# A gated mix of sliding-window attention and a token-mixing MLP: another order of the same work on the five engines

## The chip, the cores and the metric

The kernel runs on one core of a Trainium2 chip. The metric is the device time of one execution in microseconds. The core has five engines with a queue of instructions each: TensorE (PE; its weight loads are listed as PEld), ScalarE (ACT), VectorE (DVE), GpSimd (POOL) and SyncE (SP), which in this kernel only issues transfers. They wait for each other with semaphores.

## The reference

The input x has 2048 tokens of 512 features. Two branches are mixed by a gate of each token (all in bf16):

```
g = sigmoid(sum(x * gate_w))                     # one number a token
a = attention(x): qkv = x @ wqkv, 32 heads of 16; query i sees keys i-255 .. i
    o = softmax(q k / 4) v;  a = o @ wo
b = mixer(x): h = layernorm(x)                   # over the 512 features
    u = gelu(h^T w1 + b1)                        # 2048 tokens -> 1376
    y = u w2 + b2                                # 1376 -> 2048 tokens, transposed back
out = g * a + (1 - g) * b
```

## The kernel before

All work is cut into tasks of one engine each (class `Task`), some 1136 in all. A table, `PLAN`, lists for each engine the names of its tasks in the order in which that engine runs them; a digit or letter after a colon is the buffer that the task takes (one character for each). So `s2.v2:06` is a score task that writes the PSUM bank pairs 0 and 6, and `v9.0:3` starts a chain in bank 3. The function `arrange` (line 103 on) merges the five lists into one program with a clock of assumed durations (`cost_of`, line 91). Those durations change no engine's order. They do set one thing in the program: near its end, the kernel lets a POOL task wait for DVE's last operation of the kind that is marked `two`, if that one ended by the planner's clock less than a microsecond before the POOL task starts.

The names, as the prediction uses them:

- `x0.0` and so on, `xt1`, `wqk0` to `wqk3`, `wv`, `gw`, `bias`, `w1_gi`, `w2_f`, `wo`: loads on SP. `xt` are loads that transpose (line 498). `w2` lies in the same buffer as `w1`, so a `w2` load waits for the last `u` step that reads what it overwrites (line 1315). `vs` and `vz` copy values between partitions, SBUF to SBUF (lines 756 and 766); there are three `vz` buffers.
- `q`, `k`, `v`, `u`, `y`: accumulation chains of TensorE (line 708). `q0_1.2` is the step that begins with the third matmul of the chain for head group 0 and token block 1. A step is two matmuls of 512 columns, apart from the first block's q and k (one matmul) and the ends of `y`. `u` needs `h` and `w1`, `y` needs gelu's output, `w2`, and in its last two steps the attention's result.
- `kc`, `vc`, `qc`, `ub`: what takes those chains out of PSUM, on ACT or DVE.
- `s_j.v0` to `v3` and `s_j.C`: scores of block j of 128 queries, 32 rows a tile (lines 980 and 1080; C are the corners of the window). Each writes two bank pairs, and two exponentials, `e_j...0` and `.1` (ACT, line 932, 128x1024 each), empty them. `m_j...` multiplies an exponential with its mask, on DVE (lines 1012, 945) or POOL (line 571).
- `pv_j.0` to `.3`: scores times values, 32 columns a tile (line 1125). `n1_j` to `n4_j` on DVE transpose and normalise its result (`n1`, line 1216, frees the bank pair); in the plan they are written without the line, as `n11` for block 1.
- `gelu`: one stretch of four instructions on ACT (lines 1291 and 1293), with a table load before and after. `f` writes the gated result of a y chain (lines 473, 476), `o` stores it (line 1343).
- `pow`, `h`, `gl`, `gatee`, `ez`: the layer norm and the gate.

TensorE runs in four tilings: the full array for chains, 32 rows for `s`, 32 x 64 for `C`, 32 columns for `pv`. A chain may also be run in 32-column tiles (four matmuls for one). The set `THEN` names the `s` and `pv` tasks after which the chain steps stay in that tiling.

Of the kernel before, what the change touches and what calls it, by code (L numbers as in the profile page):

```python
# [90 lines left out]
def cost_of(t, e):  # L91
    c, n = t.engines[e], t.name
    if e == "PE":
        return c - 0.02 if t.mode == "s" else c * 0.738 if t.mode == "c" else c
    if e == "DVE":
        return max(0.1, c - 0.06)
    if e == "ACT":
        return c - 0.085 if n[:2] in ("vc", "kc", "ub") else c - 0.008 if n[0] == "e" else c
    if e == "POOL" and n[0] == "m" and ".C" in n:
        return c * 1.14  # L100
    return c


def arrange(tasks):
# [21 lines left out]
    while len(order) < len(tasks):  # L126
# [80 lines left out]
    pv=(7, 6, 5, 4, 3),  # L207
# [11 lines left out]
        warm:5 xta0.0.1:4 xta0.0.0:3 warmb xta0.1.1:4 xta0.1.0:5 q2_0.0:6 q3_0.0:0 k1_0.0:2 k3_0.0:3  # L219
        k0_0.0:1 q1_0.0:5 q1_0.1 k2_0.0:7 q0_0.0:4 k2_0.1 q2_0.1 k0_0.1 q0_0.1 k3_0.1 k0_0.2 q0_0.2 k1_0.1  # L220
        q0_0.3 k3_0.2 q1_0.2 k3_0.3 q1_0.3 q3_0.1 q2_0.2 k1_0.2 q1_0.4 k1_0.3 q0_0.4 k0_0.3 k3_0.4 q2_0.3
        k0_0.4 q3_0.2 q2_0.4 k2_0.2 k1_0.4 k2_0.3 k2_0.4 v1.0:1 q3_0.3 q3_0.4 s0.v0:24 v1.2 v0.0:7 q3_1.0:6
        v0.2 q3_1.2 s0.C:24 v5.0:0 k2_1.0:7 k2_1.2 v5.2 s-1.C:24 v3.0:6 v14.0:7 v14.2 s1.v3:04 biast:3 v3.2
        q1_1.0:7 q1_1.2 s1.v0:02 v2.0:6 v2.2 v12.0:4 v12.2 v4.0:5 v4.2 pv-1.0:0 s0.v1:26 k3_1.0:4 k3_1.2
        k3_2.0:5 s1.v2:06 k3_2.2 v6.0:2 q0_1.0:3 q0_1.2 v6.2 pv0.0:0 pv0.1 pv0.2 s1.v1:46 v7.0:3 v7.2
        v15.0:2 s2.v1:06 v15.2 k0_2.0:5 v13.0:4 k0_2.2 v13.2 k1_1.0:3 s1.C:06 k2_2.0:2 k2_2.2 k1_1.2
        s2.v3:06 k0_1.0:5 k0_1.2 v10.0:2 v10.2 pv1.0:0 pv1.1 pv1.2 pv1.3 s2.v0:46 pv1.4 v8.0:2 v8.2 v9.0:3
        v9.2 s2.v2:06 q2_1.0:5 k1_2.0:4 q2_1.2 s2.C:20 k1_2.2 u0.0:6 u0.2 v11.0:7 v11.2 s3.v1:40 u0.4 u0.6
        u0.8 s3.C:02 u2.0:7 u0.10 u2.2 u0.12 u2.4 s3.v2:42 pv2.0:0 u0.14 pv2.1 pv2.2 pv2.3 u2.6 u2.8
        s3.v0:24 u1.0:6 u1.2 u1.4 s3.v3:02 u1.6 u1.8 u2.10 s4.v0:42 u2.12 u1.10 u2.14 u1.12 u1.14 s4.v1:04  # L230
        pv3.0:2 pv3.1 pv3.2 pv3.3 u3.0:7 u3.2 u3.4 s5.v2:04 u3.6 u3.8 u3.10 s4.v3:20 u3.12 u3.14 u4.0:6 u4.2
        s4.v2:24 q0_2.0:7 q0_2.2 u4.4 s4.C:40 u4.6 u4.8 u4.10 s6.v0:02 u4.12 q3_2.0:7 u4.14 pv4.0:4 pv4.1
        pv4.2 pv4.3 s5.v0:02 u5.0:6 q3_2.2 u5.2 u5.4 s5.v1:42 u5.6 u5.8 q2_2.0:7 q2_2.2 s5.C:02 u5.10 u5.12
        u5.14 s6.C:04 u6.0:7 u6.2 u6.4 s6.v2:02 u6.6 u6.8 q1_2.0:6 q1_2.2 u6.10 s5.v3:04 u6.12 u6.14 u7.0:6
        s6.v1:02 u7.2 u7.4 pv5.0:4 pv5.1 pv5.2 pv5.3 s6.v3:02 u7.6 u7.8 k3_3.0:7 k3_3.2 s7.v0:04 u7.10
        pv6.0:2 pv6.1 u7.12 pv6.2 pv6.3 s7.v1:04 u8.0:7 u7.14 u8.2 s7.v3:02 u8.4 k1_3.0:6 k1_3.2 s7.C:04
        u8.6 u8.8 q0_3.0:6 s7.v2:42 q0_3.2 u8.10 u8.12 u8.14 s8.v3:20 u9.0:6 u9.2 u9.4 s8.C:04 u10.0:7 u10.2
        u10.4 s8.v1:24 u9.6 u9.8 u10.6 u9.10 s8.v0:20 u9.12 u10.8 u9.14 s8.v2:42 u10.10 pv7.0:0 pv7.1
        q1_3.0:6 u10.12 u10.14 q1_3.2 s10.v0:24 pv7.2 k2_3.0:7 k2_3.2 pv8.0:2 pv8.1 k0_3.0:6 pv8.2 pv8.3
        pv7.3 k0_3.2 q2_3.0:4 q2_3.2 q3_3.0:5 y4.0:6 y0.0:7 q3_3.2 s9.v1:02 y0.2 y0.4 y4.2 y4.4 y0.6 y4.6  # L240
        y0.8 y0.10 s9.v3:40 y0.11 y0.13 y4.8 s9.v2:02 y4.10 y4.11 y2.0:7 y2.2 s9.C:40 y2.4 y4.13 y2.6
        s9.v0:24 y2.8 y2.10 y7.0:6 y2.11 s10.C:04 y2.13 y7.2 y7.4 s10.v3:02 y7.6 y8.0:7 y8.2 s11.v3:04 y8.4
# [12 lines left out]
    """,
    ACT="""
        xtc0.0.1 xtc0.0.0 kc3_0 kc0_0 kc1_0 kc2_0 e0.v0.0:5 e0.v0.1:4 vc0 vc1 e0.C.0:3 e0.C.1:2 kc2_1 vc5
        e-1.C.1:9 e-1.C.0:8 vc14 e1.v3.0:1 e1.v3.1:b e1.v0.0:a e1.v0.1:0 vc12 gatee0 vc4 e0.v1.1:8 e0.v1.0:9
        e1.v2.0:6 e1.v2.1:7 kc3_1 vc6 e1.v1.1:2 e1.v1.0:3 e2.v1.1:4 e2.v1.0:5 vc15 kc0_2 e1.C.0:d e1.C.1:c
        kc2_2 e2.v3.0:8 vc13 e2.v3.1:9 vc10 kc1_1 e2.v0.1:0 e2.v0.0:b vc8 e2.v2.0:1 e2.v2.1:7 e2.C.1:a kc1_2  # L260
        e2.C.0:d e3.v1.1:c e3.v1.0:6 e3.C.1:e e3.C.0:f e3.v2.1:0 e3.v2.0:b ub0 e3.v0.0:7 e3.v0.1:1 e3.v3.1:a
        e3.v3.0:5 e4.v0.0:4 e4.v0.1:d ub2 e4.v1.0:1 e4.v1.1:0 ub1 gatee2 e5.v2.0:c e5.v2.1:5 e4.v3.0:6
        e4.v3.1:f e4.v2.1:e e4.v2.0:7 e4.C.1:8 e4.C.0:9 e6.v0.1:2 e6.v0.0:3 e5.v0.1:4 e5.v0.0:d e5.v1.1:0
        gatee1 e5.v1.0:1 e5.C.0:7 e5.C.1:6 e6.C.0:e ub5 e6.C.1:f e6.v2.0:a e6.v2.1:b e5.v3.0:8 e5.v3.1:g
        e6.v1.0:9 e6.v1.1:h ub6 e6.v3.0:6 e6.v3.1:7 e7.v0.0:8 e7.v0.1:g kc3_3 e7.v1.0:a e7.v1.1:6 e7.v3.0:f
        e7.v3.1:b e7.C.1:e e7.C.0:7 e7.v2.1:9 e7.v2.0:h e8.v3.1:4 e8.v3.0:5 e8.C.1:c e8.C.0:d e8.v1.0:2
# [1146 lines left out]
```

## Time and profile before

| | |
|---|---|
| three runs | 199.55, 199.56, 199.9 us; median 199.56 |
| the profiled execution | 199.2 us, its span 197.5 us |
| PE busy | 187.4 us, 95% (4008 matmuls recorded, 4040 weight loads) |
| ACT busy | 169.9 us, 86% |
| DVE busy | 157.8 us, 80% |
| POOL busy | 64.6 us, 33% |
| matmuls of chains, 512 columns, one | 380 ns from start to end; the next starts 215 ns after it |
| exponential, 128x1024, one | 1.04 us from start to end |
| DMA | 22.01 MB, most of it in the first 42 us; HBM read 15.6 MB |

The profile is one execution. A line of the chain, of the waits or of the timeline names the engine, the line of the kernel, and what is written and read (`out<-in`). In the timeline the columns are the start, the length, engine and line, operation, form and count, and in brackets the idle time before it with what ended it; neighbours of one kind are merged into one row, and the length then reaches from the first start to the last end. Matmuls overlap, so their lengths do not add up; the time from one start to the next does. Some matmul records are missing.

### The profile page before, as it was taken

To read this page: it belongs to the slowest core of one execution; us is meant where nothing else is said; L and a number is where in the kernel's file an instruction comes from. 1 tells how busy PE (TensorE), PEld (TensorE's weight loads), DVE (VectorE), ACT (ScalarE), POOL (GpSimd) and SP (SyncE) were. 2 spreads that over 40 slices of the span, in tenths; PEclk is the share of its full clock that TensorE was granted. 3 is DMA by queue.
4 is the path that set the end of the run, shared out by engine and by line. 5 is a ranking of instruction groups with operands and counts; after the bars stand their busy time and mean duration, and the time that the engine had idled before them with its cause. 6 is when DMAs were issued, how large, how long until landed. Compare 5 with 4: busy or idle time off the path is not lost.

```text
span 197.5 us, 9026 instructions
## 1 busy us (share of the span) xinstructions
PE 187.4 (95%) x4008; PEld 92.3 (47%) x4040; DVE 157.8 (80%) x340; ACT 169.9 (86%) x200; POOL 64.6 (33%) x102
## 2 busy tenths in 40 slices
PE   7999999999999999999999999899999999999994
PEld 3544344444535344456444563335345354454663
DVE  2699998799999897984767899177955775779893
ACT  3059998999899997999999899998998989899910
POOL 8922796563001122235200420222362320004520
PEclk9999999999999999999999999999999999999999
DMA  5986999942052811001496017001031002003022
GB/s 147 306 212 125 236 328 346 317 123 63 7 156 69 275 62 37 0 3 36 134 391 256 3 39 211 0 5 56 3 109 36 27 9 68 3 3 89 3 98 65
DMA packets 23444, 22.01 MB, mean 111 GB/s; under 512 B 7950, under 2 KB 21518, under 8 KB 23406
## 3 DMA queue, kind: packets, MB, share of 16 engines
q1 hardware_dynamic: 23406, 21.44, 36.1%
q8 instruction: 31, 0.51, 1.1%
q14 instruction: 7, 0.06, 0.1%
HBM read 15.61 MB, written 2.10 MB: 90 GB/s over the span
## 4 chain that ended last, share of the span: by engine, by line
PE 79%; ACT 11%; DVE 4%; issue 3%; DMA 2%; SPq 0%; ACTq 0%
PE pb L708 57%; PE ps L1125 10%; PE ps L980 9%; ACT et L932 7%; PE ps L1080 2%; ACT VA L640 2%; DMA wqkv<-in_A_wqkv_dram 2%; DVE stats L808 1%; ACT L932 1%; DVE et L1216 1%; DVE zt L1233 0%; SPq L489 0%; ACT ug L1291 0%; DVE h L824 0%; PE ps L1036 0%
## 5 line engine op out<-in xcount | busy, mean ns | idle before, releaser
L932 ACT ACTIVATE et<-ps 128x1024 bf16<-128x1024 f32 (+1 forms) x104 | 98.8, 1011 | 8.2 <-PE ps L980 5.5
L571 POOL TENSOR_SCALAR_AFFINE_SELECT et<-et 128x512 bf16<-128x512 bf16 (+3 forms) x60 | 41.6, 704 | 98.4 <-ACT et L932 65.7
L932 ACT ACTIVATE XT<-ps 128x1024 bf16<-128x1024 f32 (+1 forms) x50 | 49.1, 1028 | 1.2 <-PE ps L980 0.7
L708 PEld LDWEIGHTS <-wb 128*32 128x32 bf16 (+4 forms) x663 | 32.5, 97 | 37.0 <-issue 7.0
L708 PE MATMUL pb<-ug,wb 128*32 128x512 bf16 (+6 forms) x344 | 43.9, 365 | 0.9 <-issue 0.6
L708 PE MATMUL pb<-h,wb 128*32 128x512 bf16 (+2 forms) x301 | 41.9, 380 | 1.7 <-issue 1.7
L708 PE MATMUL pb<-XT,wqkv 128*128 128x512 bf16 (+2 forms) x166 | 31.8, 369 | 1.2 <-issue 0.8
L980 PE MATMUL ps<-QZ,KT 32*128 32x256 bf16 (+1 forms) x496 | 23.1, 265 | 0.9 <-ACT et L932 0.8
L1125 PEld LDWEIGHTS <-VA 128*32 128x32 bf16 (+1 forms) x1056 | 20.3, 97 | 6.2 <-issue 1.6
L792 DVE TENSOR_TENSOR QZ<-pb,par 128x1024 bf16<-128x1024 f32 x16 | 19.1, 1213 | 3.3 <-PE pb L708 2.4
L1125 PE MATMUL ps<-et,VA 128*32 128x128 bf16 (+2 forms) x760 | 21.7, 217 | 0.0
L1216 DVE STREAM_TRANSPOSE et<-ps 128x1024 f32<-128x1024 f32 (+1 forms) x13 | 15.7, 1207 | 4.2 <-PE ps L1125 3.7
L1012 DVE TENSOR_TENSOR et<-et,mask 128x512 bf16<-128x512 bf16 x38 | 16.9, 454 | 2.7 <-ACT et L932 2.7
L708 PEld LDWEIGHTS <-wqkv 128*128 128x128 bf16 (+1 forms) x172 | 12.0, 97 | 13.7 <-DMA wqkv<-in_A_wqkv_dram 0.9
L571 POOL TENSOR_SCALAR_AFFINE_SELECT XT<-XT 128x512 bf16<-128x512 bf16 (+1 forms) x15 | 9.8, 659 | 24.5 <-ACT XT L932 13.5
L708 PE MATMUL pb<-wo,xo 128*32 128x512 bf16 (+3 forms) x152 | 17.5, 369 | 0.4 <-issue 0.3
L980 PEld LDWEIGHTS <-KT 32*128 32x128 bf16 x496 | 7.4, 92 | 21.7 <-ACT et L932 12.1
L708 PE MATMUL pb<-wqkv,XT 128*128 128x512 bf16 x60 | 15.8, 380 | 0.6 <-issue 0.3
L1012 DVE TENSOR_TENSOR XT<-XT,mask 128x512 bf16<-128x512 bf16 x20 | 9.7, 485 | 6.4 <-ACT XT L932 6.4
L808 DVE BATCH_NORM_STATS2 stats<-xo 128x6 f32<-128x512 bf16 x16 | 10.6, 675 | 4.2 <-DMA xo<-in_A_x_dram 4.2
L1125 PEld LDWEIGHTS <-VZ 128*32 128x32 bf16 x832 | 13.2, 97 | 0.4
L1125 PE MATMUL ps<-XT,VA 128*32 128x128 bf16 (+2 forms) x296 | 12.7, 217 | 0.1
(77 smaller groups left out, 201.7 us busy)
## 6 DMA issues: line engine op xcount, KB each, us to landing
wb<-in_B_w_dram SPq DMA_DIRECT2D x18, 512.0 KB, 6.6
VZ<-VA SPq DMA_DIRECT2D x26, 70.0 KB, 2.5
xo<-in_A_x_dram SPq DMA_DIRECT2D x3, 512.0 KB, 5.0
wb<-in_B_w_dram SPq DMA_DIRECT2D x4, 352.0 KB, 7.5
out_dram<-ot SPq DMA_DIRECT2D x11, 128.0 KB, 1.8
wqkv<-in_A_wqkv_dram SPq DMA_DIRECT2D x4, 256.0 KB, 5.4
xo<-in_A_x_dram SPq DMA_DIRECT2D x2, 256.0 KB, 2.9
wqkv<-in_A_wqkv_dram SPq DMA_DIRECT2D x1, 512.0 KB, 7.7
```

The lines of the kernel that those rows point to most:

```text
L571: return nc.gpsimd.affine_select(out=out_, in_=in_, pattern=[[0, n] for n in pattern] + [[step, HB]], compare_op=op, fill=0.0, base=base_, ...
L640: return nc.scalar.activation(out_(), in_(), ACT.Copy)
L708: made.append(nc.tensor.matmul(buf(b)[c:z_, c0:c0 + w_], lhsT=lhsT[:, c:z_], rhs=rhs, start=(j == 0), stop=(j == n - 1), skip_group_check= ...
L792: lambda k=k, b=b: nc.vector.tensor_tensor(out=QZ[:, k, :, (i % NQ) * SB:(i % NQ + 1) * SB], in0=buf(b)[:, None, :].to_broadcast([P, 2, SB ...
L808: f"bs{t_}", {"DVE": 0.67}, lambda b=b, t_=t_: nc.vector.bn_stats(buf(b)[:], xo[:, t_, :]),
L932: lambda e=e, b=b, shape=shape: nc.scalar.activation(out=shape(buf(e)), in_=shape(buf(b)), func=ACT.Exp, scale=SCALE),
L980: made.append(nc.tensor.matmul(to[:, :, done:done + m], lhsT=keys(j if x == "A" else j - 1, k)[rows], rhs=q[rows], start=True, stop=True, ...
L1012: made.append(nc.vector.tensor_tensor(out=v, in0=v, in1=m.to_broadcast(list(v.shape)), op=ALU.mult))
L1080: made.append(nc.tensor.matmul(buf(b2[r // 2])[m_:m_ + HB, at:at + P], lhsT=keys(t_, k)[rows, a:a + HB], rhs=q[rows], start=True, stop=Tru ...
L1125: return lambda: nc.tensor.matmul(to(), lhsT=v() if callable(v) else v, rhs=buf(e)[rows, col:col + n], start=first, stop=last, tile_positi ...
L1216: lambda: nc.vector.transpose(out=view(buf(tr).bitcast(FP32)), in_=view(buf(o))), [last], takes=[tr], uses=[o],
```

## The change

All five lists, the buffers in them and the set `THEN` are replaced. No task is added or removed, and none changes its instructions, but 72 tasks change their engine: 33 masks go from DVE to POOL and 21 from POOL to DVE; 10 tasks go from ACT to DVE (`xtc0.0.1 xtc0.0.0 vc14 vc15 ub5 kc3_3 f1 f9 f12 f15r`) and 8 from DVE to ACT (`xtc0.1.0 xtc0.1.1 vc3 vc2 kc3_2 vc7 ub4 f14`). The lists then have 500 tasks on PE, as before; 192 on ACT (194 before), 283 on DVE (293), 87 on POOL (75) and 74 on SP. Two assumed durations of the planner change. The order of the score and pv tasks is the same but for `s5.v0`, which moves ahead of `pv4`, `pv7.3`, which moves ahead of `pv8.0`, and `pv10` and others by single chain steps.

The diff, cut to what is spoken of:

```diff
-        return c - 0.02 if t.mode == "s" else c * 0.738 if t.mode == "c" else c
+        return c - 0.01 if t.mode == "s" else c * 0.738 if t.mode == "c" else c
...
     PE="""
-        warm:5 xta0.0.1:4 xta0.0.0:3 warmb xta0.1.1:4 xta0.1.0:5 q2_0.0:6 q3_0.0:0 k1_0.0:2 k3_0.0:3
-        k0_0.0:1 q1_0.0:5 q1_0.1 k2_0.0:7 q0_0.0:4 k2_0.1 q2_0.1 k0_0.1 q0_0.1 k3_0.1 k0_0.2 q0_0.2 k1_0.1
-        q0_0.3 k3_0.2 q1_0.2 k3_0.3 q1_0.3 q3_0.1 q2_0.2 k1_0.2 q1_0.4 k1_0.3 q0_0.4 k0_0.3 k3_0.4 q2_0.3
-        k0_0.4 q3_0.2 q2_0.4 k2_0.2 k1_0.4 k2_0.3 k2_0.4 v1.0:1 q3_0.3 q3_0.4 s0.v0:24 v1.2 v0.0:7 q3_1.0:6
...
-        q1_3.0:6 u10.12 u10.14 q1_3.2 s10.v0:24 pv7.2 k2_3.0:7 k2_3.2 pv8.0:2 pv8.1 k0_3.0:6 pv8.2 pv8.3
-        pv7.3 k0_3.2 q2_3.0:4 q2_3.2 q3_3.0:5 y4.0:6 y0.0:7 q3_3.2 s9.v1:02 y0.2 y0.4 y4.2 y4.4 y0.6 y4.6
-        y0.8 y0.10 s9.v3:40 y0.11 y0.13 y4.8 s9.v2:02 y4.10 y4.11 y2.0:7 y2.2 s9.C:40 y2.4 y4.13 y2.6
...
+        warm:5 xta0.0.0:7 xta0.0.1:3 warmb xta0.1.0:3 xta0.1.1:5 k1_0.0:1 q0_0.0:0 q2_0.0:7 q2_0.1 k2_0.0:4
+        q1_0.0:2 k1_0.1 k2_0.1 q0_0.1 k0_0.0:3 q0_0.2 k1_0.2 k0_0.1 q1_0.1 k2_0.2 k1_0.3 q1_0.2 q0_0.3
+        q0_0.4 k0_0.2 q1_0.3 q1_0.4 k1_0.4 q3_0.0:6 q2_0.2 q3_0.1 k0_0.3 k0_0.4 k2_0.3 k3_0.0:5 k3_0.1
+        q2_0.3 q2_0.4 k2_0.4 k3_0.2 q3_0.2 s0.v0:20 q3_0.3 q3_0.4 k3_0.3 k3_0.4 v1.0:4 biast:3 v0.0:2 v0.2
...
+        pv7.0:2 pv7.1 u10.12 u10.14 k2_3.0:6 k2_3.2 s10.v0:04 pv7.2 q2_3.0:7 q2_3.2 pv7.3 pv8.0:0 k0_3.0:6
+        pv8.1 pv8.2 pv8.3 q1_3.0:3 q3_3.0:2 k0_3.2 q1_3.2 q3_3.2 y4.0:4 y0.0:5 s9.v1:06 y0.2 y4.2 y0.4 y0.6
+        y0.8 y0.10 y4.4 y0.11 s9.v3:26 y4.6 y0.13 y4.8 s9.v2:02 y4.10 y4.11 y2.0:5 y4.13 s9.C:60 y2.2 y2.4
...
     ACT="""
-        xtc0.0.1 xtc0.0.0 kc3_0 kc0_0 kc1_0 kc2_0 e0.v0.0:5 e0.v0.1:4 vc0 vc1 e0.C.0:3 e0.C.1:2 kc2_1 vc5
...
-        e8.v1.1:3 e8.v0.0:0 e8.v0.1:1 gatee3 e8.v2.1:8 e8.v2.0:a ub10 e10.v0.0:6 e10.v0.1:9 gelu e9.v1.0:8
...
+        xtc0.1.0 xtc0.1.1 kc1_0 kc0_0 kc2_0 e0.v0.0:a kc3_0 e0.v0.1:5 vc0 e0.C.0:9 e0.C.1:b vc1 vc2
...
+        e8.v3.0:d e8.C.0:e e8.C.1:f e8.v1.0:8 e8.v1.1:9 e8.v0.1:g e8.v0.0:h e8.v2.1:4 e8.v2.0:7 ub10
+        e10.v0.0:3 e10.v0.1:1 gelu e9.v1.1:f e9.v1.0:e e9.v3.0:0 e9.v3.1:2 e9.v2.0:d e9.v2.1:c e9.C.0:7
...
     POOL="""
-        ident masks ones blanks pow0 m0.v0.1 m0.v0.0 m-1.C.0 m-1.C.1 m0.C.1 pow1 m1.v3.1 m0.C.0 m0.v1.0
-        m0.v1.1 m1.v0.1 m1.v2.0 m1.v3.0 m1.v1.1 m1.v0.0 m1.C.1 m1.v2.1 m2.v1.1 m2.v3.0 pow2 pow3 m2.v2.0
...
+        ident blanks ones masks m0.v0.1 m-1.C.0 m-1.C.1 m1.v3.0 m1.v3.1 m0.v0.0 m0.C.1 pow1 m0.C.0 m1.v0.1
+        m0.v1.0 m0.v1.1 m1.v2.1 pow0 pow2 m1.v0.0 m1.v1.1 m1.v1.0 m1.v2.0 m2.v1.1 pow3 m2.v0.1 m2.v2.0
...
     SP="""
-        x0.0 x0.2 wqk0 wqk1 wqk2 x1.4 wqk3 gw wv xt1 bias xt3 vs0 x2.8 vs1 xt2 w1_21 x3.12 w1_00 w1_01 w1_10
-        w1_02 w1_20 vs2 w1_23 w1_12 w1_11 vz4:1 w1_03 vz8:0 vz2:2 vz3:2 w1_13 w1_22 vz5:2 wo w2_0 w2_3 vz6:1
-        vz11:2 vz7:1 w2_1 w2_4 w2_2 w2_7 w2_6 w2_5 w2_8 vz10:0 w2_9 w2_10 vz9:1 o2 o4 o7 o0 o8 vz13:1 vz12:0
...
+        x0.0 x0.2 wqk0 wqk1 wqk2 wqk3 bias gw wv xt1 x1.4 xt3 w1_03 x2.8 vs0 xt2 w1_21 vs2 vs1 w1_12 w1_00
+        x3.12 vz2:1 w1_13 vz6:2 w1_20 w1_01 w1_11 w1_02 w1_10 vz3:0 w2_0 vz7:1 w2_1 vz4:0 w2_3 w2_2 vz5:0 wo
+        w1_22 w1_23 w2_7 vz8:2 w2_4 w2_6 w2_5 vz10:0 w2_8 vz9:1 w2_9 w2_10 o4 vz11:2 o2 o0 vs13 o8 o7 o1
...
-            lambda fc=fc, fsz=fsz: nc.sync.dma_start(w2[:fsz, fc, :], B_w2[fc * P:fc * P + fsz, :]), gone, lat=2.9,
+            lambda fc=fc, fsz=fsz: nc.sync.dma_start(w2[:fsz, fc, :], B_w2[fc * P:fc * P + fsz, :]), gone, lat=3.2,
```

## The prediction

> **What bounds the kernel now.** I read the page first (engines' share, the chain that ended last), then the waits of TensorE, then timelines of the places where TensorE waits.
>
> ```profile
> span 197.5 us, 9026 instructions
> PE 187.4 (95%) x4008; PEld 92.3 (47%) x4040; DVE 157.8 (80%) x340; ACT 169.9 (86%) x200; POOL 64.6 (33%) x102
> PE 79%; ACT 11%; DVE 4%; issue 3%; DMA 2%; SPq 0%; ACTq 0%
> L932 ACT ACTIVATE et<-ps 128x1024 bf16<-128x1024 f32 (+1 forms) x104 | 98.8, 1011 | 8.2 <-PE ps L980 5.5
> ```
>
> TensorE carries 79% of the last chain. Busy time alone does not say whether it works or drains, so I worked its time out from the starts. The first chain matmul starts at 5.82 and the last ends near 194.6. A 512-column matmul follows the one before it after 0.2155 us; four 32-column ones of a tiled step share that time. In such units the kernel has 608 for the projections, u and y (131.0 us) and 35.5 us of scores and score-times-value products: 166.5. At 119.50 and 119.83 below, a score step of 0.2155 is followed after 0.33: a change of tiling costs 0.11. The order has 165 changes; each measured that way, they make 18.8 us. That leaves about 3 us, half of it scattered gaps of hundredths. TensorE really waits for only about 1.6 us after 5.82:
>
> ```profile
> 5.82 3.98 PE L708 MATMUL pb<-XT,wqkv 128*128 128x256 bf16 x25 [0.23 <-DMA wqkv<-in_A_wqkv_dram]
> 9.99 2.75 PE L708 MATMUL pb<-XT,wqkv 128*128 128x512 bf16 x12 [0.19 <-issue]
> ...
> 42.82 0.40 PE L980 MATMUL ps<-QZ,KT 32*128 32x256 bf16 x8 [0.16 <-ACT et L932]
> ...
> 119.50 0.40 PE L980 MATMUL ps<-QZ,KT 32*128 32x256 bf16 x8
> 119.83 3.54 PE L708 MATMUL pb<-ug,wb 128*128 128x512 bf16 x15
> 123.75 0.40 PE L980 MATMUL ps<-QZ,KT 32*128 32x256 bf16 x8 [0.38 <-ACT et L932]
> ```
>
> The waits I find: 0.15 near 9.7 (the fourth weight block), 0.2 at 29.6 (pv0.1 waits for a mask), 0.15 at 32.2, 0.22 at 42.8 (s2.v2 waits for the transpose n11 to free its bank), 0.12 at 122.4, 0.46 at 123.75 and 0.1 at 125.6 (after gelu), some 0.2 more. ScalarE is the partner: two exponentials follow each score step, one every 0.905 us, and in most visits TensorE's next score step starts 0.05 to 0.3 us after the exponential that frees its bank. So the two run in lock step, with no stock of slack: a later exponential, mask or copy shows on TensorE at once. The clock column of the page is 9 throughout.
>
> **What the Trainium skill says.** "TensorEngine Tiling (Array Packing)", Tiling Modes: changing the tiling mode drains TensorE; the trace agrees, at 0.11 us a change. "GPSIMD Engine Reference", Specifications: GpSimd shares its SBUF interfaces with VectorE. The trace shows POOL waiting 8.5 us for a DVE mask (L571 <- DVE et L1012), but that can be the wait the program itself puts in. "DMA: Bandwidth & Descriptors", Queues, rings and completion order: an engine's descriptors are consumed in ring order. It agrees: the packets of the fourth weight block land among and behind those of x1.4, issued just before it. "ScalarE: Activation LUTs", What ACT_TABLE_LOAD costs: back-to-back ACTIVATEs overlap by about 93 ns; the trace has 1.04 us an exponential and a pitch of 0.905.
>
> **The change part by part.** Matmuls and bytes are the same in both. The lines of `cost_of` and the `lat` of 3.2 emit nothing; they only shift the planner's clock, which decides the merging and where a POOL operation gets a wait for VectorE. What remains is order, placing and buffers.
>
> *Changes of tiling.* Counting the order with `THEN`: 165 becomes 164; tiled chain steps 72 becomes 73. -0.11 us.
>
> *Start.* The loads up to wqk2 are unchanged, so 5.82 stays. wqk3 goes ahead of x1.4 (0.5 MB, at the 306 GB/s of that slice of the page up to 1.7 us earlier), and TensorE asks for it at about 8.6: the 0.15 wait goes. Bound 0 to 0.25. The four bias loads now stand ahead of gw, wv and the transposing load xt1 on SP's queue (1.5 us of issue, 12.67 to 14.14), x1.4 after it. That load occupied the queue for 7.11 us, most of it waiting; with less ahead of it wv still lands by about 12.6, and v1.0 wants it at 13.3. 0.
>
> *First exponentials.* s0.v0 comes after 36 chain steps instead of 41 (four of 0.2155 and one of 0.431 less), at about 12.2 instead of 13.63; its copies kc1, kc0, kc2 end by 12.5, so ScalarE starts its exponentials near 12.6, not 14.08. By s1.v0 both orders have 56 chain steps, and from there on the count before every visit is equal or one step off. ScalarE's copies move too: vc2, vc3, vc7, kc3_2, ub4 to it; vc14, vc15, ub5, kc3_3 from it. From e0.v0 to s1.v1 its sum is 1.43 us more than in the old order, TensorE's 1.29 more. Against the start that is earlier by 1.4, ScalarE stands at +0.1 there, at about -0.3 before gelu.
>
> *Masks.* 33 go from DVE to POOL, 21 back: 12 x 0.336 less on DVE, 12 x 0.617 more on POOL (from the pitch of each engine's masks). With the copies and f1, f9, f12, f15r, DVE's queue is 3.2 us shorter in all. At n11 it is 0.84 ahead: the 0.22 wait at 42.8 should go (0 to 0.22). On POOL the critical stretch is from the corner masks m-1.C to m0.v1.1, which pv0.1 waits for:
>
> ```profile
> 20.69 4.32 POOL L571 TENSOR_SCALAR_AFFINE_SELECT et<-et 64x512 bf16<-64x512 bf16 x6 [2.61 <-ACT VA L640]
> 25.09 0.20 POOL L818 TENSOR_TENSOR rstd<-mv,eps 128x4 f32<-128x4 f32 x1
> 25.37 1.02 POOL L819 TENSOR_TENSOR rstd<-rstd,half 128x4 f32<-128x4 f32 x1
> 26.36 5.20 POOL L571 TENSOR_SCALAR_AFFINE_SELECT et<-et 128x512 bf16<-128x512 bf16 x8
> ```
>
> Before, 8.4 us of POOL work without a pause brought m0.v1.1 to 29.05. After, m1.v3.0, m0.v0.0 and m1.v0.1 stand in that stretch too: 10.2 us. e-1.C should end near 18.8 instead of 20.6, so m0.v1.1 starts at 29.0 again, and ends near 29.7. TensorE, 0.15 to 0.25 earlier, just waits longer: the gain of the start is lost here. I book -0.15 for the start and +0.15 here; bounds: 0 to +1.85 if POOL starts no earlier. The new masks after 45 us I book at nothing: POOL was busy for 0.2 to 4 of each 10 us, and m8.v1.1 or m15.A.1 end one microsecond or more before their pv step. If that cover were gone, each late mask costs 0.62.
>
> *Queue of transfers.* vz6 (waits for vc7, near 33) stands ahead of w1_20, w1_01, w1_11, w1_02 and w1_10 on SP. Those 2.4 MB take some 8 us at the 300 GB/s of those slices and are in by 42; u0.4 wants w1_01 at 47.5. 0. w1_22 and w1_23 go behind vz5, near 76; u8.8 wants them at 98. w2_9 and w2_10 go behind vz9, which is free two microseconds sooner because pv7.3 moves ahead of pv8.0; w2_10 was issued at 117.8 and used at 122.4 with a wait of 0.12, which should go. -0.12.
>
> *Gelu.* Its table load, 6.5 us of work and second load follow e10.v0, and s9.v3 waits for the first exponential behind them. Seven and a half chain steps stand between s9.v1 and s9.v3 in both, so the 0.46 moves with ScalarE alone: gatee3 (0.17) leaves this stretch, and ScalarE is some 0.3 ahead: -0.2, bounds -0.46 to +0.4.
>
> *After gelu.* ScalarE loses three f (0.78 each); the two or three waits of 0.1 may go: -0.1. The number of chain steps between visits is the same or one off; where s14.v1, s14.C and s15.A come one step earlier the bank is free by n113, whose queue is 2.5 us shorter.
>
> *Tail.* From pv15.2 to y15l.11 TensorE has 2.5 us of steps in both, and the chain n115 to n415 takes 2.2. f15m and o15m end it unchanged. 0.
>
> Sum: -0.11 - 0.15 + 0.15 - 0.22 - 0.12 - 0.2 - 0.1 = -0.75. Every one of some 75 visits gets a new bank or neighbour in a lock step with no slack; for new waits of the sort already seen (0.1 to 0.2, two of them) I add 0.25, an estimate. So -0.5: the profiled execution goes from 199.2 (197.5 span and 1.7 around it) to 198.7. The median of the runs is 199.56, 0.36 above it; so I predict 199.05.
>
> **The rivals.** *Nothing gained:* ScalarE and POOL hold TensorE at the mask of pv0.1 and at gelu at the same moments as before, and what TensorE saves between them it waits. For it: the slack of hundredths. Against: n11 and w2_10 don't hang on them. 199.45. *Slower, by POOL:* the ordering puts 1.84 us more POOL work ahead of m0.v1.1. If m-1.C starts no earlier than at 20.69, as it would if ScalarE's early start is lost to a copy or to a bank, m0.v1.1 ends at 31.5, pv0.1 waits 1.85 us more, and nothing gives it back: 201.2. It decides from about 19.5 on; each microsecond later is one more. *Everything gained:* all 1.6 us of waits go, and 197.9 is left; but the gelu wait hangs on work that isn't changed.
>
> **How the numbers follow.** Small gain 0.47, everything 0.04, nothing 0.22, slower by POOL or a wait like it 0.27. A measurement here can tell 0.2% (0.4 us) from no change: faster 0.51, same 0.22, slower 0.27. Range 198.1 to 200.9: it drops the floor and the full price of the slower case, which most likely comes in part, at 200 to 201. The small gain's own range is 198.3 to 199.2.
>
> **What would show it.** Right: first exponential near 12.6; no wait before the fourth block; m-1.C on POOL near 18.9 and pv0.1 held near 29.9; s2.v2 with no wait for n11; s9.v3 near 123.4. Wrong: m-1.C at 20 or later; waits of half a microsecond at visits that had 0.1; wqk1 late for TensorE's new order.

## The result: slower, and the profile after

The kernel after takes 200.35 us (median of 19 runs), the one before 199.9 beside it: a ratio of 1.0026, interval 1.0015 to 1.0037. The forecast was 199.05 and a small gain. In the profiled executions it is 200.44 us with a span of 198.7, against 199.2 with a span of 197.5.

The page of the kernel after, first its span, then the engines, then the chain that ended last by engine:

```profile
span 198.7 us, 9038 instructions
PE 188.0 (95%) x4007; PEld 92.2 (46%) x4040; DVE 154.6 (78%) x330; ACT 169.0 (85%) x198; POOL 74.5 (37%) x113
PE 70%; ACT 10%; DMA 5%; SPq 5%; DVE 4%; issue 3%; POOL 1%; ACTq 0%; POOLq 0%; DVEq 0%
```

The work is where the order put it: VectorE has 3.2 us less and POOL 9.9 us more. TensorE's busy time tells nothing, so I read the starts of single tasks out of both traces and subtracted. The third column is a mended version of the kernel after, described below.

| stretch of TensorE | before | after | mended |
|---|---|---|---|
| to the first chain matmul | 5.82 | 6.11 | 6.11 |
| from there to s1.v0 | 15.88 | 16.50 | 15.97 |
| s1.v0 to pv0.2 | 8.39 | 8.54 | 8.16 |
| pv0.2 to s2.v2 | 12.73 | 12.77 | 12.77 |
| s2.v2 to s10.v0 | 69.60 | 69.59 | 69.59 |
| s10.v0 to s9.v3 | 11.33 | 11.33 | 11.32 |
| s9.v3 to the last chain step | 70.57 | 70.72 | 70.73 |
| last chain step | 194.32 | 195.56 | 194.65 |

Of the 1.24 us between the profiles, 0.91 are there at s1.v0 and 1.06 at pv0.2. Behind 44 us only 0.15 are lost, after gelu.

The timeline of TensorE in the kernel after, at its start (start, length, engine, line, operation, form, count; in brackets the idle time before the row and what ended it):

```profile
6.11 0.50 PE L708 MATMUL pb<-XT,wqkv 128*128 128x256 bf16 x3 [0.19 <-DMA wqkv<-in_A_wqkv_dram]
7.21 5.46 PE L708 MATMUL pb<-XT,wqkv 128*128 128x256 bf16 x30 [0.59 <-ACT XT L640]
```

Three chain steps run, then TensorE stands until 7.21. The third of them began at 6.34 and takes 0.11, so the fourth, q2_0.1, waits 0.76 us: for ScalarE's copy xtc0.1.0. The timeline of ScalarE before and after:

```profile
0.79 1.28 ACT L640 ACT_TABLE_LOAD   x1 [0.79 <-PEq L1397]
4.32 1.09 ACT L640 ACTIVATE XT<-pb 128x512 bf16<-128x512 bf16 x2 [2.25 <-PE pb L646]
```

```profile
5.26 1.28 ACT L640 ACT_TABLE_LOAD   x1 [5.26 <-DVE XT L641]
6.56 1.08 ACT L640 ACTIVATE XT<-pb 128x512 bf16<-128x512 bf16 x2
```

The first block above is before, the second after. ScalarE's first table load, 1.28 us, used to run while the first loads were on their way. Now a wait for VectorE's copies (DVE XT L641) stands in front of it, and the copy that TensorE asks for at 6.45 begins at 6.56. "Perfetto Trace Analysis", Identifying Dependency Chains, in the Trainium skill, says that an instruction with several conditions may get event instructions with the other waits ahead of it. The trace agrees: a semaphore instruction of ScalarE, 17 ns long, ends at 5.23 and the table load follows.

The timeline of POOL after, which answers the one shown of before:

```profile
19.91 6.16 POOL L571 TENSOR_SCALAR_AFFINE_SELECT et<-et 64x512 bf16<-64x512 bf16 x9 [2.66 <-ACT et L932]
26.16 0.20 POOL L818 TENSOR_TENSOR rstd<-mv,eps 128x4 f32<-128x4 f32 x1
26.44 1.02 POOL L819 TENSOR_TENSOR rstd<-rstd,half 128x4 f32<-128x4 f32 x1
27.42 2.13 POOL L571 TENSOR_SCALAR_AFFINE_SELECT et<-et 64x512 bf16<-64x512 bf16 x3
29.50 1.27 POOL L571 TENSOR_SCALAR_AFFINE_SELECT XT<-XT 128x512 bf16<-128x512 bf16 x2
```

The corner masks m-1.C begin at 19.91; m0.v1.1 is the second of the last row, at 30.12: a stretch of 10.2 us without a pause, against 8.4 before. TensorE runs into its end:

```profile
30.20 0.41 PE L1125 MATMUL ps<-et,VA 128*32 128x128 bf16 x16
30.44 0.22 PE L1125 MATMUL ps<-XT,VA 128*32 128x128 bf16 x2
30.82 0.40 PE L1125 MATMUL ps<-XT,VA 128*32 128x128 bf16 x14 [0.16 <-POOL XT L571]
```

pv0.1 starts at 30.44 with two matmuls, and the other fourteen come at 30.82, behind the mask.

### The profile page after: what moved, and what is told of

The parts are those of the page before. It is cut to its first block, busy times and chain, and to the rows that moved or that the text cites. A ratio compares the mean times of both kernels' runs of the same rounds, so it can differ in the third digit from the quotient of the medians.

```text
span 198.7 us, 9038 instructions
## 1 busy us (share of the span) xinstructions
PE 188.0 (95%) x4007; PEld 92.2 (46%) x4040; DVE 154.6 (78%) x330; ACT 169.0 (85%) x198; POOL 74.5 (37%) x113
## 4 chain that ended last, share of the span: by engine, by line
PE 70%; ACT 10%; DMA 5%; SPq 5%; DVE 4%; issue 3%; POOL 1%; ACTq 0%; POOLq 0%; DVEq 0%
PE pb L708 51%; PE ps L1125 9%; PE ps L980 8%; DMA xo<-in_A_x_dram 5%; ACT et L932 4%; ACT ug L1291 2%; PE ps L1080 2%; SPq L757 2%; SPq L498 2%; ACT XT L932 2%; SPq L521 1%; SPq L756 1%; DVE stats L808 1%; ACT L932 1%; ACT L1291 1%
## 5 line engine op out<-in xcount | busy, mean ns | idle before, releaser
L932 ACT ACTIVATE et<-ps 128x1024 bf16<-128x1024 f32 (+1 forms) x97 | 90.9, 999 | 8.0 <-PE ps L980 4.5
L932 ACT ACTIVATE XT<-ps 128x1024 bf16<-128x1024 f32 x57 | 55.9, 1039 | 4.0 <-PE ps L980 2.4
L708 PEld LDWEIGHTS <-wb 128*32 128x32 bf16 (+3 forms) x651 | 32.3, 97 | 35.5 <-issue 6.3
L708 PE MATMUL pb<-ug,wb 128*32 128x512 bf16 (+5 forms) x348 | 44.0, 367 | 1.1 <-issue 0.9
L708 PE MATMUL pb<-h,wb 128*32 128x512 bf16 (+1 forms) x285 | 42.7, 380 | 1.4 <-issue 1.4
L571 POOL TENSOR_SCALAR_AFFINE_SELECT XT<-XT 128x512 bf16<-128x512 bf16 (+1 forms) x28 | 20.0, 723 | 47.8 <-ACT XT L932 38.9
L1125 PE MATMUL ps<-et,VA 128*32 128x128 bf16 (+2 forms) x688 | 19.4, 216 | 0.3 <-ACT et L932 0.3
L1012 DVE TENSOR_TENSOR et<-et,mask 128x512 bf16<-128x512 bf16 x28 | 12.6, 457 | 3.0 <-ACT et L932 3.0
L476 DVE TENSOR_SCALAR ot<-pb,c,c 128x512 bf16<-128x512 f32 (+2 forms) x12 | 8.9, 746 | 6.7 <-PE pb L708 6.7
L945 DVE TENSOR_TENSOR et<-et,mask 128x1024 bf16<-128x1024 bf16 (+1 forms) x16 | 11.4, 721 | 1.2 <-ACT et L932 1.2
(75 smaller groups left out, 199.5 us busy)
```

Of the source, the lines that this page charges most:

```text
L476: return nc.vector.tensor_scalar(out=out_, in0=in_, scalar1=scale, scalar2=bias, op0=ALU.mult, op1=ALU.add)
L571: return nc.gpsimd.affine_select(out=out_, in_=in_, pattern=[[0, n] for n in pattern] + [[step, HB]], compare_op=op, fill=0.0, base=base_, ...
L708: made.append(nc.tensor.matmul(buf(b)[c:z_, c0:c0 + w_], lhsT=lhsT[:, c:z_], rhs=rhs, start=(j == 0), stop=(j == n - 1), skip_group_check= ...
L932: lambda e=e, b=b, shape=shape: nc.scalar.activation(out=shape(buf(e)), in_=shape(buf(b)), func=ACT.Exp, scale=SCALE),
L945: return nc.vector.tensor_tensor(out=v, in0=v, in1=m[:, None, :].to_broadcast([P, n, w]), op=ALU.mult)
L1012: made.append(nc.vector.tensor_tensor(out=v, in0=v, in1=m.to_broadcast(list(v.shape)), op=ALU.mult))
```

## The experiments

Every ratio is to the kernel before on the same chip. Its medians there were 199.67 us for the first four runs, 199.56 for the control, the bank, the masks on top of it and the loads back, 199.6 for the masks alone and the attempts to beat both kernels, and 199.5 for the last run. The plan's lines in the edits are cut at their ends.

### The start

Theory: the table load behind a wait, and with it q2_0.1, is the loss. Rivals: the other order of the loads makes the first weight block land later (6.07 against 5.77 in the first two profiles); or the masks and the lock step of TensorE and ScalarE set the time whatever the start.

**Copies back.**

```diff
-        xtc0.1.0 xtc0.1.1 kc1_0 kc0_0 kc2_0 e0.v0.0:a
+        xtc0.0.1 xtc0.0.0 kc1_0 kc0_0 kc2_0 e0.v0.0:a
-        const zeros bs0:0 xtc0.0.1 xtc0.0.0 ba0 bs2:1 bs1:0 parity ba2 bs3:1
+        const zeros bs0:0 ba0 bs2:1 bs1:0 parity ba2 xtc0.1.0 xtc0.1.1 bs3:1
```

> The kernel after, with the four copies of the first block exchanged back (xtc0.0.1, xtc0.0.0 on ACT, xtc0.1.0, xtc0.1.1 on DVE, as before the change). Theory, start (ACT's table load stands behind a wait for DVE's copies, and q2_0.1 waits 0.76 us for it): the table load is at 0.8 again, xtc0.1.0 runs on DVE at 6.0 to 6.4, q2_0.1 starts at 6.5 to 6.6 instead of 7.21, and the 0.6 reaches the end: about 199.7 where the kernel after has 200.35. Rival, loads (the weights land later for the new order of loads): the first chain matmul stays at 6.1, and of the loss 0.3 stays. Rival, masks and lock step (the order behind the start sets the time): TensorE waits what it saves, at pv0.1 or later, and the time is 200.1 to 200.4.

Measured: 200.04, 1.0019 (0.9997 to 1.0041). The table load is at 0.80 and q2_0.1 has no wait of its own. But in the profiled execution the first weight block landed at 6.94, the first chain matmul came at 6.99, and the end was no earlier than after (195.53). So only some 0.3 of the median came back (200.35 to 200.04, on two chips), less than the theory's 0.6, and the landing was seen to scatter.

**Early table.**

```diff
+    add("early", {"ACT": 1.4}, lambda: nc.scalar.activation(early[:], half[:], ACT.Copy), [k0])
-        xtc0.1.0 xtc0.1.1 kc1_0 kc0_0 kc2_0 e0.v0.0:a
+        early xtc0.1.0 xtc0.1.1 kc1_0 kc0_0 kc2_0 e0.v0.0:a
```

> The kernel after, with one tiny ACT operation (128x4, of a constant) ahead of xtc0.1.0, so that the table load needs no DVE copy. All copies stay where the change put them. Theory, start: table load near 1.0, xtc0.1.0 on ACT at about 5.45 to 6.05, q2_0.1 at about 6.45 with no wait worth naming; the 0.76 reaches the end: 199.6. If the place of the copies itself (0.60 on ACT against 0.42 on DVE) and not the table load is what costs: xtc0.1.0 still ends near 7.1, time 200.3. Rival, masks and lock step: q2_0.1 is early and the time stays at 200.1 to 200.4.

Measured: 200.1, 1.002 (1.0 to 1.004). The load is at 0.80, the copy at 6.02, q2_0.1 at 6.84. About 0.25 came back, not 0.76; the chain steps from 6.20 to 7.43 took 0.21 us each and not 0.11 (see the last section). The first weight block landed at 5.73 here, with the new order of loads.

**The exchange alone, in the kernel before.**

```diff
-        xtc0.0.1 xtc0.0.0 kc3_0 kc0_0
+        xtc0.1.0 xtc0.1.1 kc3_0 kc0_0
-        zeros bs0:0 ba0 bs3:1 const bs1:0 parity ba3 xtc0.1.0 xtc0.1.1 ba1
+        zeros bs0:0 xtc0.0.1 xtc0.0.0 ba0 bs3:1 const bs1:0 parity ba3 ba1
```

> The kernel before, with the exchange of the four copies alone (xtc0.1.0, xtc0.1.1 on ACT, xtc0.0.1, xtc0.0.0 on DVE). Theory, start: the table load moves from 0.79 to about 5.3, xtc0.1.0 ends near 7.15, q1_0.1, the seventh chain step, starts at 7.2 instead of 6.60, and the kernel before becomes 0.4 to 0.7 slower. Rivals (loads; masks and lock step): no more than 0.2 slower, the second since the 0.15 wait for the fourth weight block, the mask of pv0.1 and gelu would absorb it.

Measured: 199.51, 1.0002 (0.9982 to 1.0022): no loss, against my theory. Its timelines of ScalarE and of POOL:

```profile
0.79 1.28 ACT L640 ACT_TABLE_LOAD   x1 [0.79 <-PEq L1397]
5.60 1.08 ACT L640 ACTIVATE XT<-pb 128x512 bf16<-128x512 bf16 x2 [3.53 <-PE pb L646]
```

```profile
16.72 1.28 POOL L571 TENSOR_SCALAR_AFFINE_SELECT et<-et 128x512 bf16<-128x512 bf16 x2 [5.74 <-DVE junk L860]
20.62 4.31 POOL L571 TENSOR_SCALAR_AFFINE_SELECT et<-et 64x512 bf16<-64x512 bf16 x6 [2.62 <-DVE junk L860]
```

Two things follow. The exchange doesn't put the table load behind a wait; something that came with it does. What differs is the PSUM bank: in this run ScalarE's first copy reads bank 5, which no other engine had to empty; in the kernel after it reads bank 3, which VectorE's copy had to empty first. And the kernel before has a reserve at its start: TensorE began 0.21 later here and s0.v0 was at 13.90 instead of 13.63, yet m-1.C stands at 20.62 (20.69 before), because POOL waits there for VectorE's gate work, not for the exponential. The view of before names a copy on ScalarE (ACT VA) for this wait, but in this run that copy ends at 20.93, when the mask already runs; the mask starts 0.13 behind the end of the gate work in both, and again in the kernel before with `const` first (below). After, m-1.C follows e-1.C.0 by 0.07 us, so a late start goes through. The reserve is small: with `const` first s0.v0 came 0.58 later in the kernel before, VectorE was late too, m-1.C stood at 21.20, and 0.35 reached the last chain step.

**The loads alone, in the kernel before.**

```diff
-        x0.0 x0.2 wqk0 wqk1 wqk2 x1.4 wqk3 gw wv xt1 bias xt3
+        x0.0 x0.2 wqk0 wqk1 wqk2 wqk3 bias gw wv xt1 x1.4 xt3
```

> The kernel before, with the first order of loads of the kernel after alone (wqk3 and the bias loads ahead of gw, wv and xt1, x1.4 behind xt1). Theory, start: the first chain matmul stays within 0.15 of 5.82, the wait of 0.15 for the fourth weight block goes, time the same or 0.15 less. Rival, loads: the first weight block lands at 6.07 and the first chain matmul is at 6.1; time 0.1 to 0.3 more.

Measured: 208.47, 1.0439 (1.0412 to 1.0467), which nobody expected. Its timelines of VectorE and of TensorE:

```profile
17.09 1.29 DVE L808 BATCH_NORM_STATS2 stats<-xo 128x6 f32<-128x512 bf16 x2 [9.30 <-DMA xo<-in_A_x_dram]
18.29 0.17 DVE L812 BATCH_NORM_AGGREGATE mv<-stats 128x2 f32<-128x6 f32 x1
18.49 0.69 DVE L808 BATCH_NORM_STATS2 stats<-xo 128x6 f32<-128x512 bf16 x1
19.10 3.47 DVE L792 TENSOR_TENSOR QZ<-pb,par 128x1024 bf16<-128x1024 f32 x3
```

```profile
21.58 0.61 PE L980 MATMUL ps<-QZ,KT 32*128 32x256 bf16 x8 [7.64 <-DVE QZ L792]
```

VectorE's order has the layer norm of x1.4 ahead of the copies of q. With x1.4 behind the transposing load it waits 9.3 us, and s0.v0 waits for q: it comes 7.95 us later. Another 1.4 us are lost behind it: from 22 to 25 us the granted clock was 0.50, and a 512-column matmul followed the one before it after 0.43 us, not 0.2155. The run says nothing on the first weight block's price; it shows that an order of loads can only be moved together with the order of the engine that reads them.

### The bank and the masks

**Control and bank.** The kernel after again, and with one digit changed:

```diff
-        warm:5 xta0.0.0:7 xta0.0.1:3 warmb xta0.1.0:3 xta0.1.1:5
+        warm:5 xta0.0.0:7 xta0.0.1:3 warmb xta0.1.0:4 xta0.1.1:5
```

> The kernel after, unchanged, beside the others on one chip. In its profile the table load stands near 5.3 and holds q2_0.1 at 7.2 again if its first matmul is early; s0.v0 at 13.0. If the pinned start is what makes its runs lie closer together than those of before, they do so again (all within 0.4 of each other); time 200.2 to 200.5.

> The kernel after with one digit changed: xta0.1.0 takes PSUM bank 4 instead of bank 3, which xta0.0.1 had and DVE's copy must empty first. No task changes its engine or place. Theory, bank (ACT's table load waits for DVE because the first ACT copy reads a bank that DVE had to empty): the table load is at 0.8, xtc0.1.0 runs at 5.5 to 6.1 on ACT, q2_0.1 has no wait; the same gain as from exchanging the copies back, 0.2 to 0.4: 200.0. If the shared tile that both engines write is the cause, the load stays at 5.3 and the time at 200.35.

Measured: the control 200.58, 1.0046 (1.0028 to 1.0065), a little above the range that was expected, with the load at 5.32 and q2_0.1 at 7.26; its six runs lie 0.51 apart, not within 0.4. The other bank 200.06, 1.0015 (1.0 to 1.0031). The timelines of ScalarE and TensorE with bank 4:

```profile
0.80 1.28 ACT L640 ACT_TABLE_LOAD   x1 [0.80 <-PEq L1397]
5.65 1.08 ACT L640 ACTIVATE XT<-pb 128x512 bf16<-128x512 bf16 x2 [3.58 <-PE pb L646]
```

```profile
6.01 6.53 PE L708 MATMUL pb<-XT,wqkv 128*128 128x256 bf16 x36
```

No stop any more, q2_0.1 at 6.62. The bank is the cause of the late load; the tile that both engines write is not. It is worth 0.5 in the medians of this chip (0.6 in the last chain step).

**Masks.** On top of the bank, m1.v3.0, m1.v3.1 and m1.v0.1 go behind block 0's last masks:

```diff
-        ident blanks ones masks m0.v0.1 m-1.C.0 m-1.C.1 m1.v3.0 m1.v3.1 m0.v0.0 m0.C.1 pow1 m0.C.0 m1.v0.1
-        m0.v1.0 m0.v1.1 m1.v2.1
+        ident blanks ones masks m0.v0.1 m-1.C.0 m-1.C.1 m0.v0.0 m0.C.1 pow1 m0.C.0 m0.v1.1 m0.v1.0 m1.v3.0
+        m1.v3.1 m1.v0.1 m1.v2.1
```

> As the run with the other bank, and on POOL m1.v3.0, m1.v3.1 and m1.v0.1 go behind m0.v1.1 and m0.v1.0. Theory, POOL (what is left of the loss are the masks put ahead of m0.v1.1): 1.9 us less POOL work from m-1.C to m0.v1.0, the wait of pv0.1 or pv0.2 for a mask (0.45 in the kernel after) goes, and the time falls by a further 0.2 to 0.4, to 199.6 to 199.8. If TensorE alone sets the pace there (start 0.9 later, equal number of chain steps): pv0.0 is no earlier, at most the wait of 0.45 behind it goes, and with an undisturbed start nothing changes: 200.0.

Measured: 199.48, 0.9997 (0.9985 to 1.0008): a further 0.58, and level with before. This is the mended version of the table. The timeline of TensorE there:

```profile
29.68 0.41 PE L1125 MATMUL ps<-et,VA 128*32 128x128 bf16 x16
29.91 0.40 PE L1125 MATMUL ps<-XT,VA 128*32 128x128 bf16 x16
```

pv0.1 runs in one piece. From pv0.0 to pv0.2 it is 0.56 us, with the bank alone 0.95. Of these 0.39 the profiles keep 0.19 at s2.v2, since pv1.0 waits 0.18 longer here than with the bank alone. The median fell by more; the two profiled executions lie on different sides of their medians.

**Masks alone**, the same edit in the kernel after with bank 3 kept:

> The kernel after, with the move of m1.v3.0, m1.v3.1 and m1.v0.1 behind m0.v1.1 and m0.v1.0 alone; bank 3 and the late table load stay. If start and masks are two losses that add up: q2_0.1 still at 7.2, pv0.0 at 30.2, but the wait of 0.45 at pv0.2 goes; 0.4 to 0.6 less than the kernel after, 199.9 to 200.1. If the masks only matter once the start is mended: 200.4.

Measured: 200.01, 1.0024 (1.0012 to 1.0036). q2_0.1 is still at 7.15, pv0.2 comes at 30.71 instead of 31.15. The medians don't give the size: this one is 0.57 below the control's and 0.34 below the first one of the kernel after, on other chips, and of the ratios to before only the control's (1.0046) shows a gain, the first one (1.0026) none. The traces do: from pv0.0 to pv0.2 it is 0.95 in the kernel after and 0.56 here, as with the bank mended (0.95 and 0.56). So the two losses add up: some 0.4 for the masks, some 0.5 for the bank.

**Loads back**, on top of bank and masks:

```diff
-        x0.0 x0.2 wqk0 wqk1 wqk2 wqk3 bias gw wv xt1 x1.4 xt3
+        x0.0 x0.2 wqk0 wqk1 wqk2 x1.4 wqk3 bias gw wv xt1 xt3
```

> As the run before it, with x1.4 issued ahead of wqk3 and the bias loads, as in the kernel before. If the order of the loads delays the first weight block (6.07 in the kernel after, 5.77 in before), the first chain matmul comes 0.2 to 0.3 sooner on average and the runs 0.2 faster. If its landing only scatters (5.7 to 6.9 in the profiles so far, under both orders), the time stays within 0.15 of the run before it, less the 0.15 wait for the fourth block, which comes back.

Measured: 200.08, 1.0018 (0.9999 to 1.0036), 0.6 more than without. The first weight block landed at 6.28, no earlier. The timeline of TensorE shows the price of the old order in the new one:

```profile
6.32 2.78 PE L708 MATMUL pb<-XT,wqkv 128*128 128x256 bf16 x18
9.75 2.98 PE L708 MATMUL pb<-XT,wqkv 128*128 128x512 bf16 x15 [0.64 <-DMA wqkv<-in_A_wqkv_dram]
```

The new order of chain steps asks for wqk3 at 8.94 and gets it at 9.70. Putting wqk3 ahead is a part of the change that helps, by more than the 0.15 I gave it. The first chain matmul came at 5.82, 6.03, 6.32 and 6.75 in the four profiles with the old order of loads, and at 6.01 to 6.99 in the eleven with the new one. The scatter is larger than any difference between them, so nothing supports the rival of the loads.

### Two attempts to beat both kernels

The second group of transposes took 0.62 us in all three profiles with VectorE's `zeros` ahead of `const`, and up to 1.06 in those with `const` first. So on top of bank and masks `zeros const` instead of `const zeros`; the reverse in the kernel before; and chain steps that need no late copy drawn ahead of q2_0.1:

```diff
-        k1_0.0:1 q0_0.0:0 q2_0.0:7 q2_0.1 k2_0.0:4 q1_0.0:2 k1_0.1 k2_0.1 q0_0.1 k0_0.0:3 q0_0.2
+        k1_0.0:1 q0_0.0:0 q2_0.0:7 q1_0.0:2 k0_0.0:3 q2_0.1 k2_0.0:4 k1_0.1 k2_0.1 q0_0.1 q0_0.2
```

> As the run with the other bank and the masks, and on DVE zeros ahead of const, as before the change. TensorE's first matmuls (the warming) wait for zeros: 1.04 in the three profiles with zeros first, 1.18 in the seven with const first. With zeros first the clock was full by the second group of transposes in all three profiles (0.62 us for eight), with const first only in one of seven (0.68 to 1.06, and in three of them the first chain steps take 0.21 instead of 0.11). Theory, warming: the transposes take 0.62 and all chain steps 0.11; 0.2 to 0.5 less, 199.0 to 199.3. Rival, chance: no pattern, time within 0.15 of the run before it (199.48).

> The kernel before, with const ahead of zeros on DVE as in the kernel after. Theory, warming: the first matmul at 1.18, the second group of transposes 0.7 to 1.06 long, some chain steps at 0.21; s0.v0 later by 0.3 or more, the time by 0.1 to 0.4 (the first 0.3 of a late start cost the kernel before nothing: POOL's m-1.C stands at 20.6 with s0.v0 at 13.63 and at 13.90). Rival, chance: the transposes take 0.62 and the time is 199.5 to 199.7.

> As the run with bank, masks and zeros, and q1_0.0 and k0_0.0, which need no late copy, go ahead of q2_0.1 and k2_0.0. With a full clock q2_0.1 would be asked for at 6.2 to 6.3, before xtc0.1.0 has landed (6.25 to 6.5): 0.1 to 0.25 of that wait goes, if the first weight block is early. Expected 0 to 0.2 less than that run, about 199.0, and below the kernel before.

Measured: 199.72, 1.0002 (0.9978 to 1.0025); 199.68, 1.0008 (0.9988 to 1.0028); 199.69, 1.0003 (0.9984 to 1.0021). The theory of the warming falls: with `const` first in the kernel before the transposes took 0.61, and with `zeros` first in the last of the three they took 1.06. The two attempts missed what was expected of them (199.0 to 199.3). None of them beats the mended version or the kernel before by what can be measured.

### Where the later gains went

> As the run with bank, masks, zeros and first steps, and from s9.v3 to pv9.0 every visit comes one chain step later: y4.6 goes ahead of s9.v3 and so on to y8.4 ahead of s11.v3. The tasks are the same. TensorE waits 0.55 to 0.79 for the first exponential behind gelu; one step of 0.43 now lies in that wait. Theory, ScalarE sets this stretch (in both kernels s10.v0 to s9.v3 takes 11.33, and from gelu to pv9 ScalarE runs without a gap): s9.v3 stays 11.33 behind s10.v0, its wait shrinks by 0.43, the same 0.43 is waited again before pv9.0 at the latest, and the time stays within 0.15 of that run (199.69, 1.0003 of before). So what TensorE saves ahead of gelu, by w2_10 or anything else, is lost. Rival, TensorE sets it: the step is won, pv9.0 and all behind it come 0.4 earlier, 199.3 (0.998 of before).

```diff
-        y0.8 y0.10 y4.4 y0.11 s9.v3:26 y4.6 y0.13 y4.8 s9.v2:02 y4.10 y4.11 y2.0:5 y4.13 s9.C:60 y2.2 y2.4
+        y0.8 y0.10 y4.4 y0.11 y4.6 s9.v3:26 y0.13 y4.8 y4.10 s9.v2:02 y4.11 y2.0:5 y4.13 y2.2 s9.C:60 y2.4 y2.6
...
-        y2.6 s9.v0:26 y2.8 y2.10 y7.0:4 y2.11 s10.C:60 y7.2 y2.13 y7.4 s10.v3:20 y7.6 y8.0:5 y8.2 s11.v3:60
-        y8.4 pv9.0:2
+        y2.8 s9.v0:26 y2.10 y7.0:4 y2.11 y7.2 s10.C:60 y2.13 y7.4 y7.6 s10.v3:20 y8.0:5 y8.2 y8.4 s11.v3:60
+        pv9.0:2
```

Measured: 200.75, 1.0053 (1.0035 to 1.0071), against 1.0003 for the run that it builds on, the last of the three above. The waits at s9.v3 in the timelines of TensorE, after, with bank and masks, and with the step ahead:

```profile
124.84 0.40 PE L980 MATMUL ps<-QZ,KT 32*128 32x256 bf16 x8 [0.48 <-ACT XT L932]
```

```profile
123.92 0.40 PE L980 MATMUL ps<-QZ,KT 32*128 32x256 bf16 x8 [0.63 <-ACT XT L932]
```

```profile
124.39 0.40 PE L980 MATMUL ps<-QZ,KT 32*128 32x256 bf16 x8 [0.20 <-ACT XT L932]
...
136.45 0.46 PE L1125 MATMUL ps<-XT,VA 128*32 128x128 bf16 x20 [0.34 <-ACT et L932]
```

The step of 0.43 went into the wait (0.63 to 0.20; the run that it builds on has 0.63 too), and s9.v3 stayed 11.33 us behind s10.v0 (11.32 to 11.33 in fourteen of the fifteen profiles; in the other, 11.45, TensorE waited for w2_10 on the way). So ScalarE sets s9.v3, as the theory said. With the chain matmuls between the visits counted, the saving is waited again: 0.22 before s9.v2, 0.11 before s11.v3, and 0.25 before pv9.0, where the view shows 0.34 for ScalarE.

The size of the loss was missed: the time was to stay within 0.15. Between the profiles of the two runs the last chain step moves by 1.38. Of this 0.57 is there at s10.v0, ahead of the edit; 0.29 is lost by s10.v2; and 0.51 comes in the tail, as two pauses of TensorE, inside pv14.3 and inside pv15.0. The first one:

```profile
187.23 0.50 PE L1125 MATMUL ps<-et,VZ 128*32 128x64 bf16 x8
```

Eight such matmuls take 0.23 in the run that it builds on. The pauses lie between matmuls of one task, no semaphore is waited for there, and none of the other fourteen profiles has them. Their cause is open.

## Why the prediction was wrong, step by step

- *Start: "The loads up to wqk2 are unchanged, so 5.82 stays."* This step failed. The exchange of the four xtc copies was counted in the front part and never costed, nor was the bank digit beside it. It put ScalarE's table load behind VectorE: 0.76 us at q2_0.1. The other 0.29, of the later first matmul, lies within the scatter of the landing. The 0.15 wait for the fourth block did go.
- *First exponentials.* 36 chain steps ahead of s0.v0 was right; the time follows from the start: 13.48 instead of 12.6, and 12.92 with the bank mended.
- *Masks.* The stretch was right (10.2), its start was not (19.91, forecast 18.9), so m0.v1.1 began at 30.12 and not 29.0. The late start is only a part of it: with the bank mended m-1.C still stands at 19.35. The forecast had e-1.C end near 18.8 instead of 20.6, but in the profile before e-1.C ends at 20.04, and what ends near 20.6 (20.56) is VectorE's gate work, which held m-1.C there. So the gain in sight was smaller than was reckoned. The rival *Slower, by POOL* named this and said that it decides from about 19.5 on: it came in part. I booked the masks at +0.15, as the loss of the start's gain. That pv0.0 to pv0.2 grew by nearly that (0.78 to 0.95) is luck, since there was no gain to lose; taking the three away is worth 0.39 there, whether the start is mended or not.
- *n11:* the wait for the bank at s2.v2 did go, and the 0.15 at 32.2 with it. But pv1.0, which had no wait before, now waits 0.41 (0.34 of it idle in the view), and it does so in the mended version too. The timelines of ScalarE and of TensorE after:

```profile
39.33 1.94 ACT L932 ACTIVATE et<-ps 128x1024 bf16<-128x1024 f32 x2 [0.68 <-DVE zt L1233]
```

```profile
40.41 0.41 PE L1125 MATMUL ps<-et,VA 128*32 128x128 bf16 x16 [0.34 <-ACT et L932]
```

  pv1.0 takes bank pair 6, which e2.v3.0 has to empty. That exponential takes the buffer `a`, which n10 had, and so stands 0.68 behind VectorE's n30, the last to read it. From pv0.2 to s2.v2 it is +0.04. This is the "new waits" of the sum, of which one alone is larger than the 0.25 that I gave to all.
- *Queue of transfers:* w2_10 was issued later (118.10, before 117.79), and a wait of 0.14 stayed. With start and masks mended it went, and the wait at s9.v3 grew from 0.48 to 0.63.
- *Gelu:* "ScalarE is some 0.3 ahead" was wrong. e10.v0.0 begins 0.51 behind s10.v0 in both profiles, so ScalarE carries no lead into gelu, and TensorE's wait at s9.v3 is what 11.33 us of ScalarE leave over: after, s9.v1 comes 0.13 us sooner behind s10.v0 than before, and s9.v3 does not. This step failed by its whole -0.2, and with it -0.12 of w2_10.
- *After gelu:* +0.15 instead of -0.1. Visit by visit, with the chain matmuls between them counted, it falls on two places: 0.07 by s10.v2, around pv9, and 0.08 between s13.v1 and s14.v3, around pv12. What made these two longer is open.
- *Changes of tiling* (0.11) can't be told apart from that; *Tail:* 3.1 to 3.2 us from the last chain step to the end in both, as forecast.
- *The 0.36 from profile to median* isn't a constant. In the kernel before, the time moves with the landing of the first weight block, as far as two executions show it: with `const` first the first chain matmul came at 6.75 and the time was 199.57, in the profiled one it came at 5.82 and the time was 199.2. After, q2_0.1 waits for ScalarE anyway, which can hide the landing: the 19 runs lie between 200.2 and 200.52, though the control's six lie further apart. This is a part of why the medians differ by less (0.45) than the profiles (1.24). Another is the median of before, 199.9 beside the result and 199.5 to 199.67 in the experiments; beside the control the medians differ by 1.02.

With bank and masks mended the sum of all other edits is 0.9997 of before. *Nothing gained* describes them best, though not by the mask of pv0.1 that it named: what n11 and the wait at 32.2 gave went into the wait at pv1.0, and what w2_10 gave into the wait behind gelu. What made the kernel after slower were one bank and three masks in the first 31 us.

## What to carry to other kernels

When tasks change their engine, cost the first instruction of each engine too: what it waits for also holds the table load that comes with it, and a PSUM bank that another engine has to empty is enough. Ask of each early stretch what pins it: before, POOL waited there for VectorE, and some 0.25 us of a late start were hidden; after, it hung on the chain from TensorE through ScalarE and hid nothing. A gain of TensorE ahead of a stretch that ScalarE set end to end was no gain here.

## What the runs showed that I had not expected

- TensorE's first matmuls run at half the speed for a time that differs from run to run: in the profiles, a chain step of 256 columns took 0.21 us up to 7.43 (early table), 6.75 (bank) or 6.67 us (bank and masks), and 0.11 from the first one at 5.82 before. In the first of these it cost 0.6 us. "TensorE: Matmul & The Clock Gate", Part 1, of the Trainium skill describes a clock at half rate that is released after a busy window of some 3.4 us, and a window that runs freely. The trace agrees in the halved rate (0.21 against 0.11). From the first matmul (1.04 to 1.18) to full speed it was under 4 us before, whose second group of transposes took 0.62 from 4.97 on, and 6.3 us with the early table: no more than two such windows, by an estimate from the page's figure. Neither of the two orders of `zeros` and `const` fixed the moment.
- "ScalarE: Activation LUTs", What ACT_TABLE_LOAD costs, gives 1283 ns for the load; the trace has 1.28. That the load runs behind the waits of the first activation, at 5.26 instead of 0.79, only the trace shows.
- The last packet of the first weight block, issued at 1.8 us, landed anywhere from 5.73 to 6.94 us.
